# Chunked attention and a wide feed-forward on one core: dense turned weights, quarter-size value tiles, and keys and queries interleaved by GpSimd ahead of the transpose

## The chip, the cores and the metric

The kernel runs on one core of a Trainium2 chip. The core has TensorE (PE in the profile, with PEld for its weight loads), VectorE (DVE), ScalarE (ACT), GpSimd (POOL) and SyncE (SP), each of which works through its own instructions in program order and waits on semaphores for the others. DMAs are issued from the POOL and SP queues. The metric is device time in microseconds: 256.27 us is the median of three runs before the change (255.0 to 256.6).

## The reference

There are 4 batches, 8 heads, 768 positions and a head size of 64. Attention works in chunks of 32 queries. Each chunk sees 8 memory slots, 16 positions to its left, its own 32 and 8 to its right, that is 64 keys:

```
scores = (q_c @ [mem_k, k_ctx].T) / 8
a      = exp(scores - max) / sum
out_c  = a @ [mem_v, v_ctx]
```

The 8 heads side by side make a row x of 512 features. It is then normalized and passed through a feed-forward layer of width 2048: `x + relu(((x - mean) / std * g) @ w1) @ w2`. Inputs and output are float32; the kernel multiplies in float16.

## The kernel before

The unit of attention work is a tile t of 128 tokens (four chunks, all heads); a batch has 6 tiles, 24 in all. The feed-forward takes two tiles at a time, a "unit" u of 256 tokens, 12 units in all. While PE does the feed-forward of unit u, the attention of tiles 2u+2 and 2u+3 is woven in between.

**One attention tile** goes through these helpers.
- `qk(t)`: `qk_products` makes 32 small matmuls (line 294) of 64 rows by 32 columns, whose positions in the array repeat with period four, into one PSUM bank. `below_max` (lines 304, 305) takes the maximum and subtracts it on VectorE, `weights` (line 311) takes the exponential on ScalarE, into `P`.
- `pt(t)`: four transposes of `P` (line 321), then two copies (line 330), one on VectorE and one on ScalarE. They put the two 64-row halves into `PTz`, a tile twice as large whose other half is zero, so that a 128-row matmul can serve two chunks at once.
- `val(t)`: `val_products` makes 16 matmuls (line 336) of 128 rows by 64 columns against `V`, into the PSUM tile `two`. `tokens` (lines 345, 346, 352) divides by the sum and gives the mean on VectorE, `shift` (line 359) subtracts the mean on GpSimd into `xn`.
- `turn_x(t)`: four transposes of `xn` (line 388), and a multiplication by g on VectorE into `xT` (line 394). `root(t)`: a sum of squares on ScalarE and, on GpSimd, the reciprocal root `rstd` (lines 378, 382).

**The feed-forward of a unit** is 8 calls of `up` (line 407: 8 matmuls of 256 columns each, then a ReLU on ScalarE, line 415) and 7 of `down7` (line 472: 8 matmuls of 256 columns, then an addition on VectorE, line 479). `down7` computes a 2 by 2 block product with 7 products in place of 8, for which VectorE makes sums of activations (`r_sum`, line 468, four per unit) and, once, sums of weights (`w2_sum`, line 453). Unit u holds up(u) and down7(u-1). The first units use the plain `down` (line 423).

**Keys and queries** of a batch are loaded by two DMAs of the POOL queue (`load_octets`, line 117, called by `load_kq`) into `raw` tiles: 96 partitions of 8 positions each, all heads. They have to be turned, head size onto partitions, before `qk` can use them. `turn` (line 232) takes a pair of heads: 16 transposes of 96 rows by 64 columns, one head in the upper half of the array's columns and the other in the lower. `to_stream` (line 245, two copies) puts keys into `KT`, and `to_rows` (line 252, one copy) puts queries into `QD`. `turn_k` and `turn_q` do it for the head pair j, so a batch has four of each. The values of a batch come in small DMAs of the POOL queue (`load_v_group`, lines 125 and 130, for batches 0 and 1; `load_v_head`, lines 139 and 144, later) straight into `V`, and `v_shared` and `v_mem` (lines 161, 166) copy rows within `V` by DMAs of the SP queue.

**The order of work** is written out by hand. Up to unit 2 it is a list of calls ("the prologue": batch 0, both first units, then `down(0, 0)` to `down(0, 7)` with the four `turn_k` of batch 1 between them). From unit 2 on, a plan holds for each unit u and step 0 to 15 what is called ahead of that step's dense product; even steps end with `up(u, step/2)`, odd ones with `down7(u-1, step//2)`, or with `down(1, step//2)` in unit 2. Step 15 has no dense product from unit 3 on. All engines get their instructions in the order of this plan, so a GpSimd copy or a DMA issue stands in the POOL queue where the plan calls it.

In the plan, unit u has qk of its two tiles at steps 0 and 2, pt at 4 and 7, val at 6 and 9, turn_x at 11 and 14, root at 12 and 14 (in unit 2 everything but turn_x and root is four steps later). The keys and queries of batch b (2 or 3) are loaded at step 5 of unit 3b-4 and turned at steps 8, 9, 12 and 13 of units 3b-3 and 3b-2.

**PSUM:** from unit 2 on, scores, transposes and turns share the two banks `one` in turn (`slot`); `up` has two banks, `down7` two, `two` takes the last two.

## Time and profile before

| | |
|---|---|
| median of three timed runs | 256.27 us (255.0 to 256.6) |
| span of the profiled execution, first to last instruction | 255.3 us |
| mean granted TensorE clock | 0.971 |
| busy: PE, PEld, DVE, ACT, POOL | 235.8, 192.9, 176.0, 122.0, 94.4 us |
| instructions | 8286 |

The profile gives the profiled execution's span and no time around it; the median of the timed runs is 1.0 us above that span. Units without turns last 16.2 to 16.7 us in it (for instance 197.3 to 213.9), units with turns 18.6 to 19.1 us (143.5 to 162.1).

A row of a group gives line, engine and operation, out<-in, partitions x elements and type, the count, then the busy time and the mean ns of one, and the idle time of the engine ahead of them with what ended it. A row of the timeline gives start and length in us, then the same names, and in brackets the idle time before it and its releaser. Matmuls overlap in the pipeline, so the distance from one group's start to the next group's start tells more than a group's length.

### The profile page before, as it was taken

Reading aid. Unit: us, or ns where it says so; the run is one execution under the profiler, and the core shown is the slowest. Engines: PE = TensorE matmul, PEld = TensorE weight load, DVE = VectorE, ACT = ScalarE, POOL = GpSimd, SP = SyncE. Lnnn points to the kernel's source line nnn. Section 1 sums busy time; section 2 is a strip of 40 time slices with the busy share of each in tenths; the row PEclk is TensorE's granted clock in tenths of the full one; section 3 lists DMA queues with packets and bytes.
Section 4 is the critical chain, followed back from the end, with each engine's and each line's share of the span. In section 5 each row is a group of like instructions: output and inputs, shape, how many; then the busy total and the mean of one; then the engine's idle time right before and its main releaser. Section 6 shows DMA issues by size and latency. Waiting matters only on the chain.

```text
span 255.3 us, 8286 instructions
## 1 busy us (share of the span) xinstructions
PE 235.8 (92%) x3611; PEld 192.9 (76%) x3611; DVE 176.0 (69%) x390; ACT 122.0 (48%) x226; POOL 94.4 (37%) x164
## 2 busy tenths in 40 slices
PE   8697978999999989999999999999999999999983
PEld 7353656786566778888789878878889888899972
DVE  7535574757597598697696687687775966856272
ACT  2225456578345445545644464554555444653310
POOL 8394332016991296741322638712113022121000
PEclk9959995999999999999999999999999999999999
DMA  6989999932999987974196569933101002011022
GB/s 82 139 94 207 208 215 206 202 27 17 60 172 143 198 103 46 103 101 70 65 155 114 104 42 58 135 70 61 57 3 51 34 3 82 3 43 43 3 82 83
DMA packets 45816, 23.50 MB, mean 92 GB/s; under 512 B 33492, under 2 KB 41140, under 8 KB 45732
## 3 DMA queue, kind: packets, MB, share of 16 engines
q0 software_dynamic: 40672, 14.70, 49.2%
q1 hardware_dynamic: 5108, 8.28, 11.1%
q8 instruction: 28, 0.46, 0.8%
q14 instruction: 8, 0.07, 0.1%
HBM read 29.46 MB, written 6.29 MB: 140 GB/s over the span
## 4 chain that ended last, share of the span: by engine, by line
PE 69%; DVE 18%; ACT 4%; DMA 4%; issue 3%; DVEq 0%; ACTq 0%; POOLq 0%
PE upb L407 28%; PE dnb L472 18%; PE dnb L423 5%; DVE RS L468 4%; PE one L232 4%; DMA raw<-in_k_dram 4%; PE two L336 4%; DVE nmx L304 3%; DVE sub L305 3%; DVE xs L479 3%; PE one L294 2%; PE one L388 2%; ACT PTz L330 2%; PE upb L542 2%; DVE T L453 1%
## 5 line engine op out<-in xcount | busy, mean ns | idle before, releaser
L407 PE MATMUL upb<-xT,w1c 128*128 128x256 f16 x768 | 101.3, 276 | 1.2 <-DVE xT L394 0.9
L407 PEld LDWEIGHTS <-w1c 128*128 128x128 f16 x768 | 80.0, 115 | 5.5 <-DVE xT L394 1.4
L415 ACT ACTIVATE rT<-upb 128x512 f16<-128x512 f32 x92 | 54.6, 593 | 56.9 <-PE upb L407 56.7
L479 DVE SCALAR_TENSOR_TENSOR xs<-dnb,rstd,xs 128x256 f32<-128x256 f32 x70 | 33.7, 481 | 24.3 <-PE dnb L472 23.1
L359 POOL TENSOR_SCALAR xn<-xs,nmean 128x512 f16<-128x512 f32 x18 | 12.4, 691 | 76.6 <-DVE nmean L352 36.8
L472 PEld LDWEIGHTS <-RS 128*128 128x128 f16 x320 | 30.0, 98 | 4.3 <-DVE RS L468 0.7
L311 ACT ACTIVATE P<-sub 128x512 f16<-128x512 f32 x24 | 15.2, 632 | 35.0 <-DVE sub L305 34.9
L472 PE MATMUL dnb<-T,RS 128*128 128x256 f16 x240 | 30.9, 273 | 0.8 <-DVE xs L479 0.8
L472 PEld LDWEIGHTS <-rT 128*128 128x128 f16 x240 | 23.1, 98 | 2.6
L472 PE MATMUL dnb<-w2c,rT 128*128 128x256 f16 x160 | 20.6, 273 | 0.0
L394 DVE TENSOR_TENSOR xT<-one,g_col 128x512 f16<-128x512 f16 x22 | 15.1, 687 | 7.4 <-PE one L388 7.2
L232 PEld LDWEIGHTS <-raw 96*64 96x64 f16 (+2 forms) x576 | 13.5, 110 | 8.6 <-issue 5.8
L378 POOL TENSOR_SCALAR veps<-ssq 128x1 f32<-128x1 f32 x24 | 5.4, 227 | 36.2 <-ACT sq L374 36.0
L374 ACT ACTIVATE sq<-xs,nmean 128x512 f16<-128x512 f32 x24 | 17.3, 719 | 0.2
L346 DVE CUSTOM_DVE_ANT_1 xs<-two,rec 128x512 f32<-128x512 f32 x24 | 16.6, 691 | 0.8
L468 DVE TENSOR_TENSOR RS<-rT 128x1024 f16<-128x1024 f16 x20 | 13.7, 686 | 4.9 <-ACT rT L415 4.9
L423 PE MATMUL dnb<-w2c,rT 128*128 128x512 f16 x64 | 16.3, 380 | 0.0
L336 PEld LDWEIGHTS <-PTz 128*64 128x64 f16 x384 | 8.5, 114 | 10.2 <-ACT PTz L330 6.0
L304 DVE TENSOR_REDUCE nmx<-one 128x8 f32<-128x512 f32 x21 | 14.4, 684 | 2.1 <-PE one L294 2.0
L305 DVE TENSOR_TENSOR sub<-one,nmx 128x512 f32<-128x512 f32 x21 | 14.5, 691 | 0.7
L336 PE MATMUL two<-V,PTz 128*64 128x65 f16 x384 | 11.1, 202 | 4.1 <-ACT PTz L330 3.3
L382 POOL TENSOR_TENSOR rstd<-veps,mhalf 128x1 f32<-128x1 f32 x24 | 13.3, 554 | 2.0
(118 smaller groups left out, 321.4 us busy)
## 6 DMA issues: line engine op xcount, KB each, us to landing
out_dram<-xs SPq DMA_DIRECT2D x23, 256.0 KB, 2.0
raw<-in_k_dram POOLq DMA_DIRECT2D x4, 768.0 KB, 9.8
raw<-in_q_dram POOLq DMA_DIRECT2D x3, 768.0 KB, 14.8
w1c<-in_moe_w_ch_dram POOLq DMA_DIRECT2D x2, 1024.0 KB, 13.3
w2c<-in_moe_w_ch_dram POOLq DMA_DIRECT2D x4, 512.0 KB, 22.7
V<-in_v_dram POOLq DMA_DIRECT2D x16, 77.0 KB, 3.1
V<-in_v_dram POOLq DMA_DIRECT2D x15, 56.0 KB, 4.1
V<-memv SPq DMA_DIRECT2D x6, 120.0 KB
```

What stands on the lines that cost most here:

```text
L232: nc.tensor.matmul(out=pv[64 * par : 64 * par + 64, n * r : n * r + n], lhsT=src[lo : lo + n, heads + par, r, :], rhs=identity[lo : lo + n ...
L304: nc.vector.tensor_reduce(out=m, in_=scores, axis=AX.X, op=ALU.max)
L305: nc.vector.tensor_tensor(out=s.rearrange("p (c k) -> p c k", c=8), in0=scores, in1=free(m, 0, [[1, 8], [0, 64]]), op=ALU.subtract,)
L336: nc.tensor.matmul(out=two[64 * gg : 64 * gg + 64, 128 * h : 128 * h + 65], lhsT=PTz[t % 3][:, 4 * (h // 2) + 2 * gg + h % 2, :, :], rhs=V ...
L346: nc.vector.tensor_tensor_reduce(out=x.rearrange("p (h d) -> p h d", h=H), in0=free(two, 0, [[128, 8], [1, 64]]), in1=free(r, 0, [[1, 8], ...
L374: nc.scalar.activation(out=sq, in_=xs[t % 9], func=ACTF.Square, bias=nmean[t % 6], scale=1.0, accum_out=ssq[i],)
L407: nc.tensor.matmul(out=p[:, 256 * hb : 256 * hb + 256], lhsT=free(w1c[hc // 8][:, dt, :], 512 * (hc // 4 % 2) + hc % 4, [[4, 128]]), rhs=x ...
L415: nc.scalar.activation(out=o, in_=i, func=ACTF.Relu)
L423: nc.tensor.matmul(out=p, lhsT=rT[u % 2][:, hc, 128 * i : 128 * i + 128], rhs=w2c[hc // 4][:, hc % 4, :], start=(hc == 0), stop=(hc == 15),)
L468: nc.vector.tensor_tensor(out=RS[k], in0=a, in1=b, op=op)
L472: nc.tensor.matmul(out=p[:, 0:256], lhsT=left[:, n, :], rhs=right(n), start=(n == 0 and not add), stop=(n == 7), skip_group_check=add,)
L479: nc.vector.scalar_tensor_tensor(out=x, in0=p[:, 0:256], scalar=rstd[t % 9], in1=x, op0=ALU.mult, op1=ALU.add,)
```

## The change

1. `PTz` (three tiles of 128 x 1024 with zeros) becomes `PT` (three of 128 x 512). `pt` ends with one copy of all 128 partitions on ScalarE. The memsets of the zeros go.
2. `val_products` makes 32 matmuls of 64 rows by 32 columns in place of 16 of 128 by 64. Their positions in the array repeat with period four, as those of `qk_products` do.
3. In the plan, the scores of tile t+2 stand right behind val of tile t (steps 4 and 8), that is, a unit earlier than before; pt follows at steps 11 and 14 and val only in the next unit.
4. For batches 1 to 3, `mix` copies a pair of heads on GpSimd from `raw` into one of four `mixed` tiles (96 partitions, 8 x 128 elements, the two heads next to each other). `turn_mixed` then makes 8 transposes of 96 rows by all 128 columns in place of 16 by 64 columns.
5. The plan moves what belongs to it: batch 1 has four mixes behind its first value loads and four more between the `down` calls, where three of its four `turn_q` stand now as well; `w2_sum` is spread out; the loads of batches 2 and 3 are called at step 0 of unit 3b-4, their mixes from step 12 of that unit to step 7 of the next, all their turns at steps 1, 2, 5, 6, 10, 11, 13 and 15 of unit 3b-3. The value loads start at step 6; `load_v_ends`, `v_shared` and `v_mem` follow at steps 6 and 10 of unit 3b-2.

```diff
-    PTz = [sb.tile([128, 16, 2, 32], FP16, name=f"PTz{i}") for i in range(3)]
+    PT = [sb.tile([128, 4, 128], FP16, name=f"PT{i}") for i in range(3)]
+    mixed = [sb.tile([128, 8, 128], FP16, name=f"mixed{i}") for i in range(4)]
...
+    def mix(b, which, j):
+        src, m = raw[RAW[b][which]], mixed[(2 * j + which) % 4]
+        nc.gpsimd.tensor_copy(
+            out=m[0:96, :, :].rearrange("p r (a d) -> p r a d", a=2),
+            in_=free(src[0:96], 1024 * j, [[64, 8], [512, 2], [1, 64]]),
+        )
+
+    def turn_mixed(which, j):
+        p, src = slot(), mixed[(2 * j + which) % 4]
+        pv = as16(p)
+        for r in range(8):
+            nc.tensor.matmul(
+                out=pv[:, 96 * r : 96 * r + 96], lhsT=src[0:96, r, :],
+                rhs=identity[0:96, 0:96], is_transpose=True, start=True, stop=True,
+            )
+        return pv
...
     def turn_k(b, j, engine):
-        to_stream(KT[b % 2], turn(raw[RAW[b][0]], 2 * j), j, engine)
+        pv = turn_mixed(0, j) if b else turn(raw[0], 2 * j)
+        to_stream(KT[b % 2], pv, j, engine)
     def turn_q(b, j, engine):
-        to_rows(b, turn(raw[RAW[b][1]], 2 * j), j, engine)
+        to_rows(b, turn_mixed(1, j), j, engine)
...
-        z = PTz[t % 3]
-        src = pv.rearrange("p (c q) -> p c q", c=16)
-        for y in range(2):
-            rows = slice(64 * y, 64 * y + 64)
-            copy_on(engines[y])(out=z[rows, :, y, :], in_=src[rows, :, :])
+        copy_on(engine)(out=PT[t % 3].rearrange("p j q -> p (j q)"), in_=pv)
...
             for gg in range(2):
-                nc.tensor.matmul(
-                    out=two[64 * gg : 64 * gg + 64, 128 * h : 128 * h + 65],
-                    lhsT=PTz[t % 3][:, 4 * (h // 2) + 2 * gg + h % 2, :, :],
-                    rhs=V[b % 2][:, 2 * tt + gg, h, 0:65],
-                    start=True, stop=True, tile_position=(0, 64 * gg),
-                )
+                for y in range(2):
+                    rows, col = slice(64 * y, 64 * y + 64), 64 * gg + 32 * y
+                    q0 = 64 * gg + 32 * (h % 2)
+                    nc.tensor.matmul(
+                        out=two[col : col + 32, 128 * h : 128 * h + 65],
+                        lhsT=PT[t % 3][rows, h // 2, q0 : q0 + 32],
+                        rhs=V[b % 2][rows, 2 * tt + gg, h, 0:65],
+                        start=True, stop=True, tile_position=(64 * y, col),
+                    )
...
     for g in range(2):
         load_v_group(1, g)
+    for j in range(2):
+        mix(1, 0, j)
+        mix(1, 1, j)
...
+    mem_cols(KT[1], memKT[:, 4:8, :], True)
     down(0, 0)
     val(5, "A")
+    turn_k(1, 0, "A")
+    mix(1, 0, 2)
     turn_x(4)
     down(0, 1)
-    mem_cols(KT[1], memKT[:, 4:8, :], True)
+    turn_q(1, 0, "A")
+    mix(1, 1, 2)
+    w2_sum(0)
     down(0, 2)
     turn_x(5)
+    turn_k(1, 1, "A")
+    mix(1, 0, 3)
     down(0, 3)
-    root(4)
+    turn_q(1, 1, "A")
+    mix(1, 1, 3)
+    w2_sum(1)
     for g in range(6, 9):
         load_v_group(1, g)
-    turn_k(1, 0, "V")
     down(0, 4)
+    root(4)
+    turn_k(1, 2, "V")
+    down(0, 5)
     root(5)
     for g in range(9, NG):
         load_v_group(1, g)
-    turn_k(1, 1, "A")
-    down(0, 5)
-    turn_k(1, 2, "V")
+    turn_q(1, 2, "A")
     down(0, 6)
-    turn_k(1, 3, "A")
+    turn_k(1, 3, "V")
     down(0, 7)
...
-    for j in range(4):
-        at(2, j, turn_q, 1, j, "AV"[j % 2])
+    at(2, 0, turn_q, 1, 3, "A")
+    at(2, 4, qk, 6)
+    at(2, 4, qk, 7)
+    at(2, 7, pt, 6)
+    at(2, 8, pt, 7)
...
+            for step, t in ((4, a), (8, c)):
+                at(u, step, val, t)
+                if t + 2 < 2 * NP:
+                    at(u, step, qk, t + 2)
+            at(u, 8, turn_x, a)
+            at(u, 7, root, a)
+            at(u, 12, turn_x, c)
+            at(u, 11, root, c)
+            if u < NP - 2:
+                at(u, 11, pt, a + 2)
+                at(u, 14, pt, c + 2)
...
-        at(u0 - 1, 5, load_kq, b)
+        at(u0 - 1, 0, load_kq, b)
+        for n, (j, which) in enumerate((j, w) for j in range(4) for w in range(2)):
+            w, step = ((-1, 12), (-1, 13), (0, 0), (0, 1), (0, 3), (0, 5), (0, 6), (0, 7))[n]
+            at(u0 + w, step, mix, b, which, j)
+            step = (1, 2, 5, 6, 10, 11, 13, 15)[n]
+            if which:
+                at(u0, step, turn_q, b, j, "A")
+            else:
+                at(u0, step, turn_k, b, j, "V")
         for h in range(H):
+            w, step = divmod(6 + 2 * h, 16)
             for part in range(2):
-                at(u0, 2 * h, load_v_head, b, h, part)
+                at(u0 + w, step + part, load_v_head, b, h, part)
...
-        at(u0 + 1, 15, mem_cols, KT[b % 2], memKT[:, 4 * b : 4 * b + 4, :], True)
+        at(u0 + 1, 0, mem_cols, KT[b % 2], memKT[:, 4 * b : 4 * b + 4, :], True)
```

(`u0` is 3b-3. In unit 2 the values of tiles 6 and 7 stand at steps 9 and 11, the scores of tiles 8 and 9 at steps 12 and 15, and their pt at steps 2 and 3 of unit 3.)

More of the change, by code (lines that the diff above doesn't have):

```diff
@@ L315, in qk, with pt @@
         weights(t)
-    def pt(t, engines="VA"):
+    def pt(t, engine="A"):
         p = slot()
@@ L595 @@
     nc.vector.tensor_copy(out=memv0, in_=memv32)
-    for i in range(2):
-        nc.vector.memset(PTz[i][64:128, :, 0, :], 0.0)
-        nc.vector.memset(PTz[i][0:64, :, 1, :], 0.0)
     nc.vector.memset(mhalf, -0.5)
```

39 lines of the change are left out of this document (14 added, 25 removed).

## The prediction

> **What bounds the kernel now.** I read the busy times first, then PE's timeline of one unit with turns (unit 6, then the start of 7), then the waits of PE from 90 to 230 us.
>
> ```profile
> PE 235.8 (92%) x3611; PEld 192.9 (76%) x3611; DVE 176.0 (69%) x390; ACT 122.0 (48%) x226; POOL 94.4 (37%) x164
> ```
> ```profile
> 157.18 1.04 PE L472 MATMUL dnb<-w2c,RS 128*128 128x256 f16 x8
> 158.14 0.53 PE L232 MATMUL one<-identity,raw 96*64 96x96 f16 x16
> 158.61 1.06 PE L407 MATMUL upb<-xT,w1c 128*128 128x256 f16 x8
> 159.60 0.53 PE L232 MATMUL one<-identity,raw 96*64 96x96 f16 x16
> 160.06 1.05 PE L472 MATMUL dnb<-T,rT 128*128 128x256 f16 x8
> ...
> 166.70 1.04 PE L407 MATMUL upb<-xT,w1c 128*128 128x256 f16 x8
> 167.57 1.04 PE L472 MATMUL dnb<-T,RS 128*128 128x256 f16 x8
> 169.19 0.44 PE L336 MATMUL two<-V,PTz 128*64 128x65 f16 x16 [0.58 <-ACT PTz L330]
> 169.56 1.07 PE L407 MATMUL upb<-xT,w1c 128*128 128x256 f16 x8
> ```
> ```profile
> PE two L336 <- ACT PTz L330: 3.3, 7, 0.6
> PE upb L407 <- DVE xT L394: 0.9, 1, 0.9
> PE one L294 <- DVE KT L214: 0.7, 2, 0.3
> ```
>
> PE is busy 92% of the span. A dense group that another dense group follows takes 0.87 us from start to start (166.70 to 167.57). So PE's order is nearly the time, and there are three things to gain: what small groups cost, what entering them costs, and the waits. Two turns with two dense groups take 157.18 to 160.06, 2.88 us, less 2 x 0.87: **0.57 us a turn**, of which 0.09 is in the dense group ahead (157.18 to 158.14 is 0.96) and 0.03 behind. The val group takes 0.37 us (169.19 to 169.56); with the same entry and exit it costs about 0.50. The waits that PE shows from unit 3 to unit 11 add up to 3.3 + 0.9 + 0.7 = 4.9 us.
>
> **The change part by part.**
>
> *Values.* Twice as many matmuls, each a quarter of the array. The nearest row is scores, which have this count, size and pattern of positions:
>
> ```profile
> 33.80 0.41 PE L294 MATMUL one<-KT,QD 64*32 64x64 f16 x32
> 34.05 0.45 PE L294 MATMUL dnb<-KT,QD 64*32 64x64 f16 x32
> 34.43 0.48 PE L232 MATMUL dnb<-identity,raw 80*64 80x80 f16 x16
> ```
>
> One takes 0.38 us alone (34.05 to 34.43), and the 16 larger matmuls took 0.37: nothing gained or lost by the split itself (0.1 either way kept for the range, 24 tiles). But of two such groups in a row the first takes only 0.25 (33.80 to 34.05). With val at 0.50 and scores at 0.35 + 0.13, the two apart cost 0.98; side by side 0.25 + 0.35 + 0.13 = 0.73. The plan has 16 such pairs (units 2 to 9): 16 x 0.25 = **-4.0 us**.
>
> *Turns.* Eight transposes by all columns in place of 16. The trace has no 96 x 128 one that streams 96 columns. Matmuls of 128 columns of weights that stream 64 take 0.94/32 = 29 ns (below); the dense ones that stream 256 take 0.87/8 = 109 ns. A line through both gives 42 ns for 96.
>
> ```profile
> 5.40 1.11 PE L548 MATMUL upb<-zeros 128*128 128x64 f16 x32
> 6.34 1.89 PE L542 MATMUL upb<-zeros 128*128 128x512 f16 x8
> ```
>
> So 8 x 42 = 0.34 us, and no entry and exit, since the shape of the array stays. I take 0.35, 24 turns: 24 x 0.22 = **-5.3 us**. Bounds: at the 29 ns of the shorter stream 0.23 us, at the 109 ns of the longer 0.87, which would lose 7 us; the line lies far nearer the first.
>
> *Waits.* Val now comes two steps behind its pt in unit 2 and eight from unit 4 on, and the first scores of a batch four steps behind mem_cols, so all **-4.9 us** can go. What is late next is worked out below. The copy on VectorE leaves its queue:
>
> ```profile
> L330 DVE COPY PTz<-one 64x512 f16<-64x512 f16 x19 | 7.8, 410 | 0.6
> L346 DVE CUSTOM_DVE_ANT_1 xs<-two,rec 128x512 f32<-128x512 f32 x24 | 16.6, 691 | 0.8
> L304 DVE TENSOR_REDUCE nmx<-one 128x8 f32<-128x512 f32 x21 | 14.4, 684 | 2.1 <-PE one L294 2.0
> L305 DVE TENSOR_TENSOR sub<-one,nmx 128x512 f32<-128x512 f32 x21 | 14.5, 691 | 0.7
> L245 DVE COPY KT<-one 128x576 f16<-128x576 f16 x10 | 7.5, 748 | 0.0
> L245 DVE COPY KT<-one 128x192 f16<-128x192 f16 x10 | 3.6, 357 | 1.3 <-PE one L232 1.1
> ```
>
> ScalarE keeps its copy, only larger in partitions, so this is nothing on PE's path. In a unit without turns I walked the plan with these durations: behind val, VectorE needs about 1.2 us (0.69 for line 346 and three short ones) plus 0.68 + 0.69 for the scores, and the bank of scores is wanted again three steps or 3.1 us later. That fits, by 0.3 us.
>
> *Two banks in a unit with turns.* Units 3 and 6 now hold eight turns each. The same walk there finds PE three times at a bank that VectorE hasn't emptied: at step 6 (the subtraction of step 4, 0.5 us), at step 10 (that of step 8, 0.6) and at step 11 (the key copies of step 10, 0.75 + 0.36, 0.8 us). Together 1.9, taken as 2.0 us a unit: **+4.0 us**. Below, none if VectorE runs ahead; above 6, if mixes delay VectorE as well.
>
> *Mixes.* GpSimd has no such copy in the trace. Its nearest rows are a fill of the same type, and, for what VectorE does to GpSimd, three of the timeline:
>
> ```profile
> L529 POOL MEMSET V<- 128x1536 f16 x1 | 1.4, 1402 | 0.0
> ```
> ```profile
> 56.70 0.19 POOL L378 TENSOR_SCALAR veps<-ssq 128x1 f32<-128x1 f32 x1 [5.17 <-ACT sq L374]
> 90.42 0.68 DVE L468 TENSOR_TENSOR RS<-rT 128x1024 f16<-128x1024 f16 x1
> 90.53 0.63 POOL L378 TENSOR_SCALAR veps<-ssq 128x1 f32<-128x1 f32 x1
> ```
>
> 1402/1536 is 0.91 ns an element; 1024 elements and some 0.15 us to start are 1.1 us. Bounds: half of that if two elements go at once, twice if reading and writing add up. 90.53 shows that GpSimd can be held: the same line takes 0.19 us at 56.70, and here it ended with VectorE's sum. The Trainium skill, "SBUF — State Buffer", section "Who interferes with whom", says that a VectorE instruction with two SBUF inputs and a GpSimd instruction that reads SBUF lock each other out whole. The row agrees for one direction; the other, a mix that holds a sum, no row shows, and by the page each collision would cost VectorE up to one mix.
>
> *Where POOL's queue decides.* A mix waits for its DMA to land, and everything behind it in POOL's queue waits too.
>
> ```profile
> 33.18 0.77 POOL L117 DMA_DIRECT2D raw<-in_q_dram  x1 [5.04 <-PE one L232]
> 59.39 1.03 PE L423 MATMUL dnb<-w2c,rT 128*128 128x512 f16 x4
> 62.35 0.79 POOL L125 DMA_DIRECT2D V<-in_v_dram  x1
> 76.31 0.77 POOL L117 DMA_DIRECT2D raw<-in_k_dram  x1
> ```
> ```profile
> raw<-in_q_dram POOLq DMA_DIRECT2D x1, 768.0 KB, 19.3
> raw<-in_k_dram POOLq DMA_DIRECT2D x1, 768.0 KB, 10.6
> raw<-in_q_dram POOLq DMA_DIRECT2D x1, 768.0 KB, 14.8
> raw<-in_q_dram POOLq DMA_DIRECT2D x1, 768.0 KB, 10.5
> ```
>
> Batch 1's queries land at 33.2 + 19.3 = 52.5; the first four mixes end near 56, inside the idle 5.2 us ahead of 56.70: free. From 62.35 to 76.31 POOL issues value loads nearly without a gap. The next four mixes stand behind the first three pairs of these, at about 66.3 to 70.7. PE comes to turn_k(1, 2) at about 66.3 (from `down(0, 0)` at 59.39 on, by the prices above) and waits for the first until 67.4: **+1.1 us**. And all loads behind them move by 4 x 1.1: although batch 2's keys are called five steps earlier, they are issued not at 76.3 but near 80, right behind the last value loads. Of the landing times I take those of this place (second and third row, with the DMAs full), less 1 us since part of the traffic is past: keys at 89.6 to 90.7, queries 94.4 to 95.7. PE enters unit 3 at about 89.0 (71.5 at the end of the prologue, then 16 x 0.87 of dense work and 3.6 of attention). There turn_k(2, 0), at 89.9, waits for a mix that ends near 91.2, and turn_q(2, 0) for one that ends near 96.2. Less the work in between, PE stands still 1.4 + 3.5: **+4.9 us**. Bound below: with the last row (batch 3's queries, issued into idle queues) 1.3 us. Batch 3 itself, called at the start of unit 5 and mixed twelve steps (11.5 us) later, is in time by that row. Behind the wait in POOL's queue stand root(7) and xn of tile 8, which are due only at the end of unit 3.
>
> *Sum.* -4.0 - 5.3 - 4.9 + 4.0 + 1.1 + 4.9 = **-4.2 us** on the span of 255.3. The page gives no time around the span; the median of the timed runs is 1.0 above it, and I carry that: 256.3 - 4.2 = **252 us**. About 1% is what a measurement of this kernel can tell from no change.
>
> **Rivals.**
>
> *The clock halves behind the wait.*
>
> ```profile
> 32.20:39.00 6.80, 4.36 (x177) 3.56 (x176) 5.12 (x10) 4.46 (x10) 2.03 (x3) 1.00 1.08 215
> 39.00:45.90 6.90, 6.30 (x80) 4.83 (x81) 3.56 (x11) 3.62 (x7) 1.31 (x2) 0.51 1.16 204
> 18.50:25.40 6.90, 5.15 (x57) 2.49 (x55) 3.67 (x9) 3.19 (x5) 3.32 (x5) 1.00 1.17 207
> ```
>
> With PE idle for 2.4 of 6.8 us (first row) the granted clock is 0.51 in the next 6.9; idle for 1.75 (last row) it stays 1.00. A wait of 4.9 us within 6.5 would likely be over the limit. The price is half of 6.8 us, 3.4, less some 0.8 of bank waits that a slower PE doesn't meet: 2.6 us, 252 + 2.6 = **255 us**. Against it: the wait comes in two pieces, and a boundary between them could leave each short. The Trainium skill, "TensorE: Matmul & The Clock Gate", section "What's actually happening", speaks of a free-running window that must be idle; by that, pieces of 1.4 and 3.5 us may not trip it. The rows here halve the clock at less than one whole idle window, so I trust them more.
>
> *The loads land in time.* At the lower bound the wait is 1.3 in place of 4.9: **248 us**, with no halved clock. For it: fewer transfers share the DMAs than in 76 to 92 us of before. Against it: the last value loads go right ahead.
>
> *GpSimd's copy is dear.* The case on the other side. At 2.2 us a mix, the four behind the value loads last to 75, the loads of batch 2 are issued near 84.6, and its queries are ready near 101.5 in place of 96: +5.5, then the halved clock +2.6, a late xn in unit 6 (+1.3) and sums held by longer mixes (+1): 252 + 10 = **262 us**. It decides from about 1.6 us a mix, with the clock halved. For it: three-level source addresses and a shared port. Against it: 0.91 ns an element in the row.
>
> *Whole turns aren't cheaper.* If a transpose of 96 columns takes 60 to 70 ns, a turn costs what it did: 252 + 4 = **256 us**.
>
> **How the numbers follow.** Forecast 252 (251 to 253.5): 0.30. Halved clock 255: 0.23. Loads in time 248: 0.20. Dear copies 262: 0.17. Turns no cheaper 256: 0.10. Faster by over 1% means under 253.7: the forecast, the loads in time and a little of the halved clock, 0.52. Slower means over 258.8: the dear copies and a little more, 0.20. Within 1%: 0.28. The range takes in 248 with 2 us for bank waits that don't come, and up to 261, short of the whole of the dear case: 246 to 261.
>
> **What would show it.** In the after profile: the scores groups right behind val start 0.25 us after it, and val has no row that waits for PT. Turns (eight matmuls of 96 x 128) take 0.34 us to the next start. Copies on POOL last 1.1 us. Units 4, 5, 7 and 8 last about 15.4 us, unit 6 about 20. The waits of PE name the mixed tiles at the start of unit 3, and POOL waits there for raw's DMA. The clock rows show whether 0.5 follows. The prediction is wrong if mixes take over 1.6 us, if units without turns stay above 16, or if unit 3 shows no wait.

## The result, and the profile after

The changed kernel takes **253.06 us** (median of 11 runs, 250.6 to 253.8); the kernel before took 255.40 (median of 11 runs too). The ratio is 0.988, with a 95% interval of 0.985 to 0.992: the gain is clear of the noise, and small. The profiled execution took 253.46 us and spans 251.5. The forecast was 252 us, within 246 to 261.

The page of the changed kernel, busy times and GpSimd's new copies:

```profile
PE 230.8 (92%) x3803; PEld 194.6 (77%) x3803; DVE 166.6 (66%) x358; ACT 119.6 (48%) x228; POOL 120.7 (48%) x188
L261 POOL COPY mixed<-raw 96x1024 f16<-96x1024 f16 x24 | 26.5, 1134 | 11.2 <-DMA raw<-in_q_dram 5.7
```

PE lost 5 us of work and is still busy for 92%. POOL gained 26 us. PE's timeline in unit 6 (start, length, and the idle time before it with its releaser in brackets):

```profile
145.21 0.51 PE L271 MATMUL one<-identity,mixed 96*128 96x96 f16 x8
145.55 1.04 PE L492 MATMUL dnb<-w2c,rT 128*128 128x256 f16 x8
...
148.61 0.42 PE L356 MATMUL two<-V,PT 64*32 64x65 f16 x32
148.87 0.44 PE L315 MATMUL one<-KT,QD 64*32 64x64 f16 x32
149.24 1.06 PE L427 MATMUL upb<-xT,w1c 128*128 128x256 f16 x8
...
152.62 0.50 PE L271 MATMUL one<-identity,mixed 96*128 96x96 f16 x8 [1.09 <-DVE sub L326]
```

A turn takes 0.34 us (145.21 to 145.55), and the scores start 0.26 behind the values (148.61 to 148.87), both as forecast. The waits of PE from 55 us to the end (total, times, longest):

```profile
PE one L271 <- POOL mixed L261: 4.3, 2, 2.3
PE two L356 <- DMA V<-memv: 2.4, 3, 1.3
PE one L271 <- DVE sub L326: 1.7, 3, 1.1
...
PE one L271 <- DVE KT L246: 0.6, 2, 0.3
```

No row names PT any more. In its place stand mixes (copies by `mix` on GpSimd, into a `mixed` tile), and a releaser that no step of the prediction has: `V<-memv`, the memory rows that `v_mem` copies into V.

**Where the time went**, from the starts of PE's groups in both timelines. Up to the first `down`: 59.39 to 57.58, -1.8 us. From there to unit 3: +2.9, of which about 1 us (an estimate: two score groups at 0.48) is the scores of two tiles that stand ahead of unit 3 now. Unit 3 (90.29 to 112.91, 22.6 us): +3.5. Units 4 and 7, which have lost their turns: -3.5 each. Unit 6 (20.5 us): +1.9. Units 5 and 8: +0.5 together. From unit 9 to the end: -3.8, since these scores are no longer among the last. Together -3.8 us on the span.

The first of these was not in the sum. VectorE's timeline in the start, before and after:

```profile
19.66 0.42 DVE L330 COPY PTz<-dnb 64x512 f16<-64x512 f16 x1 [2.78 <-PE dnb L321]
20.00 0.67 DVE L304 TENSOR_REDUCE nmx<-dnb 128x8 f32<-128x512 f32 x1
```
```profile
16.60 0.68 DVE L325 TENSOR_REDUCE nmx<-dnb 128x8 f32<-128x512 f32 x1
```

Before, VectorE's half of the weights' copy stood in its queue ahead of the second tile's maximum, and waited 2.78 us for PE to turn the first tile's weights. The whole copy is on ScalarE now, and the maximum is 3.4 us earlier. The start itself varies from profile to profile (last section). Of the nine profiles whose start is of the same kind, the kernel before alone has its first `up` at 28.7 us, and the eight with the whole copy on ScalarE at 26.7 to 27.5.

Now the places where PE waits for mixes in the changed kernel: PE, then GpSimd, then windows of time. A row of a window gives its start, end and length, the busy time (and instructions) of PE, PEld, DVE, ACT and POOL, PE's granted clock, the busy share of the DMA engines and the GB/s that they moved.

```profile
63.31 1.03 PE L443 MATMUL dnb<-w2c,rT 128*128 128x512 f16 x4
66.28 0.72 PE L271 MATMUL one<-identity,mixed 96*128 96x96 f16 x8 [1.94 <-POOL mixed L261]
...
95.22 0.51 PE L271 MATMUL one<-identity,mixed 96*128 96x96 f16 x8 [2.33 <-POOL mixed L261]
```
```profile
64.69 4.48 POOL L261 COPY mixed<-raw 96x1024 f16<-96x1024 f16 x4
...
94.13 1.04 POOL L261 COPY mixed<-raw 96x1024 f16<-96x1024 f16 x1 [2.90 <-DMA raw<-in_q_dram]
```
```profile
59.40:66.20 6.80, 4.94 (x49) 2.77 (x46) 5.85 (x9) 5.27 (x11) 6.63 (x11) 1.00 0.83 53
66.20:69.90 3.70, 3.62 (x22) 2.05 (x23) 1.02 (x2) 0.52 (x1) 3.70 (x6) 0.54 0.02 4
88.00:96.00 8.00, 5.67 (x89) 4.48 (x87) 6.77 (x10) 4.93 (x11) 3.42 (x6) 1.00 0.68 156
```

In the prologue PE needs 2.97 us from 63.31 on instead of 0.87, a wait of 2.1, and then works at about half the clock for 3.7 us (0.54). In unit 3 GpSimd waits for the queries' DMA, and PE for GpSimd, but the clock stays at 1.00.

### The profile page after: what moved, and what is told of

The parts are those of the page before. It is cut to its first block, busy times and chain, and to the rows that moved or that the text cites. A ratio compares the mean times of both kernels' runs of the same rounds, so it can differ in the third digit from the quotient of the medians.

```text
span 251.5 us, 8668 instructions
## 1 busy us (share of the span) xinstructions
PE 230.8 (92%) x3803; PEld 194.6 (77%) x3803; DVE 166.6 (66%) x358; ACT 119.6 (48%) x228; POOL 120.7 (48%) x188
## 4 chain that ended last, share of the span: by engine, by line
PE 59%; DMA 15%; DVE 10%; POOL 9%; issue 3%; ACT 2%; DVEq 0%; POOLq 0%; ACTq 0%
PE upb L427 25%; PE dnb L492 19%; DMA V<-memv 6%; DMA raw<-in_q_dram 6%; DMA raw<-in_k_dram 4%; POOL V L126 3%; PE upb L562 2%; PE two L356 2%; POOL V L131 2%; POOL mixed L261 2%; DVE xs L366 2%; PE one L408 2%; DVE xs L499 2%; PE one L271 2%; PE one L315 2%
## 5 line engine op out<-in xcount | busy, mean ns | idle before, releaser
L427 PE MATMUL upb<-xT,w1c 128*128 128x256 f16 x768 | 99.3, 275 | 0.1
L427 PEld LDWEIGHTS <-w1c 128*128 128x128 f16 x768 | 81.1, 115 | 3.3 <-issue 0.6
L435 ACT ACTIVATE rT<-upb 128x512 f16<-128x512 f32 x92 | 53.4, 593 | 38.4 <-PE upb L427 38.0
L379 POOL TENSOR_SCALAR xn<-xs,nmean 128x512 f16<-128x512 f32 x18 | 13.7, 759 | 38.3 <-PE upb L427 20.7
L261 POOL COPY mixed<-raw 96x1024 f16<-96x1024 f16 x24 | 26.5, 1134 | 11.2 <-DMA raw<-in_q_dram 5.7
L488 DVE TENSOR_TENSOR RS<-rT 128x1024 f16<-128x1024 f16 x20 | 15.1, 756 | 9.9 <-ACT rT L435 9.9
L271 PEld LDWEIGHTS <-mixed 96*128 96x128 f16 x192 | 10.9, 100 | 10.2 <-POOL mixed L261 5.1
L325 DVE TENSOR_REDUCE nmx<-one 128x8 f32<-128x512 f32 x21 | 14.4, 685 | 5.6 <-PE one L315 5.6
L443 PE MATMUL dnb<-w2c,rT 128*128 128x512 f16 x64 | 17.7, 401 | 0.0
L271 PE MATMUL one<-identity,mixed 96*128 96x96 f16 x160 | 10.3, 208 | 6.7 <-POOL mixed L261 4.3
L126 POOL DMA_DIRECT2D V<-in_v_dram x16 | 11.8, 737 | 6.9 <-DMA w1c<-in_moe_w_ch_dram 3.2
## 6 DMA issues: line engine op xcount, KB each, us to landing
raw<-in_q_dram POOLq DMA_DIRECT2D x3, 768.0 KB, 15.9
```

The source lines that it names most:

```text
L126: nc.gpsimd.dma_start(out=V[b % 2][72 : 72 + n, g, :, 0:64], in_=dram(v, b * H * HS + (64 * g + 16) * D, [[64, n], [HS, H], [1, 64]]),)
L261: nc.gpsimd.tensor_copy(out=m[0:96, :, :].rearrange("p r (a d) -> p r a d", a=2), in_=free(src[0:96], 1024 * j, [[64, 8], [512, 2], [1, 64]]),
L271: nc.tensor.matmul(out=pv[:, 96 * r : 96 * r + 96], lhsT=src[0:96, r, :], rhs=identity[0:96, 0:96], is_transpose=True, start=True, stop=True,)
L427: nc.tensor.matmul(out=p[:, 256 * hb : 256 * hb + 256], lhsT=free(w1c[hc // 8][:, dt, :], 512 * (hc // 4 % 2) + hc % 4, [[4, 128]]), rhs=x ...
L435: nc.scalar.activation(out=o, in_=i, func=ACTF.Relu)
L443: nc.tensor.matmul(out=p, lhsT=rT[u % 2][:, hc, 128 * i : 128 * i + 128], rhs=w2c[hc // 4][:, hc % 4, :], start=(hc == 0), stop=(hc == 15),)
```

## The experiments

In the table, "from the first `down`" is the span less the start of that product in the same profile; it leaves the start out, whose length varies (last section). Each ratio is against the runs of the kernel before that were taken along with that kernel's runs (their medians lie between 254.8 and 255.4 us).

| kernel | median us | ratio to before (95%) | from the first `down`, us |
|---|---|---|---|
| before | 255.40 | 1 | 195.9 |
| changed | 253.06 | 0.988 (0.985 to 0.992) | 193.9 |
| e_denseonly | 251.56 | 0.985 (0.979 to 0.991) | 193.6 |
| e_rawturns | 251.02 | 0.979 (0.971 to 0.988) | 192.1 |
| e_apart | 256.29 | 1.002 (0.998 to 1.007) | 197.3 |
| e_mixtwice | 270.19 | 1.056 (1.048 to 1.064) | 212.7 |
| e_memrows | 252.54 | 0.989 (0.983 to 0.996) | 194.1 |
| e_mixfirst | 254.97 | 0.998 (0.993 to 1.002) | 192.9 |
| e_loads2 | 257.36 | 1.004 (1.000 to 1.009) | 201.2 |
| e_ahead | 253.80 | 0.995 (0.991 to 0.999) | 194.1 |
| e_order | 257.84 | 1.010 (1.006 to 1.014) | 199.5 |
| e_rawmem | 247.54 | 0.967 (0.961 to 0.972) | 188.9 |
| e_hybrid | 247.32 | 0.969 (0.964 to 0.975) | 187.5 |

The profiled runs of e_mixfirst (251.96 us, the fastest of ten) and of e_rawmem and e_hybrid are among the fastest of theirs, those of e_loads2, e_order and e_mixtwice (258.65, 259.06, 271.81) among the longest; the ratio is the measure, the last column tells where.

The theory: the dense weights and the values beside the scores pay, and the mixes give back what the cheaper turns earn, because GpSimd has them in one queue with the DMA issues. The first rival: the loads alone are late, and with them sooner the whole change pays. The second: VectorE's two banks and the lock of the shared port.

### The parts, one at a time

**e_denseonly**, the kernel before with the first two points of the change:

```diff
-            copy_on(engines[y])(out=z[rows, :, y, :], in_=src[rows, :, :])
...
+        copy_on(engine)(out=PT[t % 3].rearrange("p j q -> p (j q)"), in_=pv)
...
```

`val_products` is that of the change, the order of work that of before.

> The kernel before with one part of the change alone: the turned weights dense, one ScalarE copy in place of two copies by ScalarE and VectorE, values by quarter-size tiles. The plan, the turns and the loads are those of before. Theory (a late copy, not the tile size, is what this part removes): in the start the second unit's maximum no longer stands behind VectorE's copy, so the first product of the feed-forward starts up to 1.7 us sooner, and PE's 3.3 us of waits for the zero-padded weights fall to about 1.5, because the one copy of all rows takes longer than the half did: 250 to 252.5 us, 0.98 to 0.99 of before. Rival (the recorded working: the copy that leaves VectorE is nothing on PE's path, and the waits go only because values stand two units behind their weights): within 0.5 us of before, 0.998 to 1.002.

Measured 0.985: this part alone is worth as much as the whole change, within the intervals. Part of the difference between the two profiles is the varying start, but the last column of the table leaves that out: 193.6 us against 195.9 before. A row of its waits of PE:

```profile
PE two L335 <- ACT PT L326: 1.4, 5, 0.3
```

The waits for the weights fall from 3.3 to 1.4 us although val stands where it stood. The theory of a late copy holds, and the recorded "nothing on PE's path" falls: the copy that the prediction left out of its sum was on the path.

**e_rawturns**, the changed kernel without mixes:

```diff
-        pv = turn_mixed(0, j) if b else turn(raw[0], 2 * j)
-        to_stream(KT[b % 2], pv, j, engine)
+        to_stream(KT[b % 2], turn(raw[RAW[b][0]], 2 * j), j, engine)
...
-            at(u0 + w, step, mix, b, which, j)
...
```

`turn_q` is changed alike, and the eight mixes of batch 1 go too.

> The changed kernel with the copies on GpSimd left out and its turns made as before, 16 transposes of 96 rows by 64 columns straight from the loaded tiles, in the places of the changed plan. Theory: the 24 turns cost 0.57 in place of 0.34 us, +5.5, while the waits for the copies (1.9 and 2.3), the half clock in the prologue (1.7) and the sums that a copy holds (1.1 at unit 6) go, -7.0; the net is near -1.5, span about 250, ratio 0.98 to 0.985, so the copies earn nothing as they are placed. Rival (whole turns are the larger gain): the span rises by 2 us or more, ratio 0.995 or above, because something else is late in their place.

```profile
145.08 0.53 PE L233 MATMUL one<-identity,raw 96*64 96x96 f16 x16
145.54 0.63 PE L426 MATMUL upb<-xT,w1c 128*128 128x256 f16 x4
```

Its turn takes 0.46 us and makes the dense groups beside it 0.1 longer, the old price. With 24 dearer turns it is no slower than the changed kernel: 251.0 us against 253.1, though the two intervals touch (0.971 to 0.988, 0.985 to 0.992). So **as placed, the mixes earn nothing**. That they cost more than they save is clear from e_rawmem below: with the memory rows sooner and no mixes it has 0.961 to 0.972, and e_memrows and e_ahead, with the memory rows sooner and the mixes, have 0.983 to 0.996 and 0.991 to 0.999.

**e_apart**, the changed kernel with the scores one dense product behind the values:

```diff
-                    at(u, step, qk, t + 2)
+                    at(u, step + 1, qk, t + 2)
```

> The changed kernel with the scores of units 3 to 8 issued one dense product after the values instead of right behind them. By the recorded price (0.25 us a pair) PE loses 0.25 x 12 = 3 us: 256 us, 1.000 of before. By the traces of both kernels the product ahead of a narrow group is 0.10 us longer and the one behind it 0.03 us, so parting a pair costs one more entry and exit, 0.13 us x 12 = 1.6 us: 254.6 us, 0.995. In the trace: scores at 0.34 to 0.35 us instead of 0.37, and the product between at 0.99 to 1.00 us instead of 0.87 to 0.90.

The time is nearer the recorded price; its rows in unit 4 are not:

```profile
117.81 1.04 PE L492 MATMUL dnb<-w2c,rT 128*128 128x256 f16 x8
118.77 0.42 PE L356 MATMUL two<-V,PT 64*32 64x65 f16 x32
119.13 1.07 PE L427 MATMUL upb<-xT,w1c 128*128 128x256 f16 x8
...
120.13 0.41 PE L315 MATMUL one<-KT,QD 64*32 64x64 f16 x32
120.47 1.05 PE L492 MATMUL dnb<-T,RS 128*128 128x256 f16 x8
```

Five groups, from the dense one ahead of val to the one behind the scores, take 0.96 + 0.36 + 1.00 + 0.34 + 0.89 = 3.55 us, against 0.97 + 0.25 + 0.38 + 0.90 + 0.87 = 3.37 in unit 4 of the changed kernel. The second pair gives 0.14, and the whole unit 0.34 for its two. So a pair is worth **0.17 us**, not 0.25. The plan has 14 pairs, in units 3 to 9 (in unit 2 the scores stand away from the values), and they make 2.4 of the 3.4 us between the two profiles. The rest is waits: PE's for mixes are 6.0 us here (3 times) against 4.3, and those for memory rows 1.7 against 2.4.

**e_mixtwice**, each mix made twice:

```diff
     def mix(b, which, j):
+        mix_once(b, which, j)
+        mix_once(b, which, j)
```

> The changed kernel with each of the 24 mixes made twice, so 27 us more of copies on GpSimd. If mixes set PE's pace wherever they stand (the recorded rival of a dear copy, 262 us at 2 to 2.2 us a mix): 261 to 266 us, 1.02 to 1.04 of before. If they count only where GpSimd is late (four mixes in the prologue, some three in unit 3) and are hidden in unit 6: 4.5 + 3 us and some clock, 259 to 261 us, 1.014 to 1.022. If GpSimd's time is idle time: under 255 us.

```profile
PE one L275 <- POOL mixed L265: 11.3, 4, 6.0
PE one L412 <- POOL xn L383: 5.2, 2, 3.2
```

270 us, above all three: 17 us more for 24.5 us of copies (51.0 against 26.5). GpSimd's time isn't idle time. Of these, 7 us are in the waits for mixes and 5.2 in a new one, for xn, which GpSimd computes behind the mixes; the rest isn't placed.

### The late transfers

**e_memrows** issues the memory rows sooner, and nothing else:

```diff
+    v_mem(1)
     mem_cols(KT[1], memKT[:, 4:8, :], True)
     down(0, 0)
...
-    at(2, 0, v_mem, 1)
...
-        at(u0 + 1, 10, v_mem, b)
+        at(u0, 2, v_mem, b)
```

> The changed kernel with one thing moved: the DMAs that copy the memory rows into V are called at step 2 of the unit that turns the batch (batch 1: ahead of the first `down`), not behind the shared rows eight steps after it. Theory: these DMAs, of 192 small packets, land last before the first values of each batch; PE's waits for them (0.8, 0.25 and 1.3 us in units 2, 5 and 8, 2.4 in all) go and nothing else is late, so the span falls from 251.5 to about 249.2 and the ratio to the kernel before from 0.988 to about 0.979. Rival: the shared rows, which are issued later now, land as late; then the same waits stay under the other name and the ratio stays at 0.986 to 0.988.

The waits for the rows are gone, and PE's largest wait is a new one, while GpSimd waits for batch 1's queries (PE, then POOL):

```profile
69.56 0.82 PE L271 MATMUL one<-identity,mixed 96*128 96x96 f16 x8 [5.21 <-POOL mixed L261]
```
```profile
56.06 3.03 POOL L261 COPY mixed<-raw 96x1024 f16<-96x1024 f16 x3 [6.16 <-DMA raw<-in_q_dram]
```

In the changed kernel these mixes start at 52.80. That the rows' transfer, issued into the same stretch, is what held the queries up is the likely reading; no run separates it. The prologue took back what units 2, 5 and 8 gained.

**e_mixfirst** puts value groups 3 to 5 behind the second four mixes:

```diff
-    for g in range(3, 6):
-        load_v_group(1, g)
...
-    for g in range(6, 9):
+    for g in range(3, 9):
         load_v_group(1, g)
```

> The changed kernel with the value loads of groups 3 to 5 of batch 1 moved behind the second four GpSimd copies, so that the order in POOL's queue changes and its total does not. Theory (POOL's queue decides): the wait of 1.9 us among the `down` products goes, and the half clock behind it (3.4 us at 0.5, worth 1.7) goes too, but batch 2's keys and queries are issued at the same time as now, near 78.6 and 79.4, so PE comes to unit 3 some 3.6 us earlier and waits there for the copies 2.3 + 3.6 = about 6 us; the span falls by under 1 us, and the half clock may come at unit 3 instead. Rival (the prologue's wait is a loss of its own): the span falls by 3 to 3.6 us, to about 248, ratio 0.974.

The prologue's wait and its halved clock are gone, and PE comes to the first values of unit 2 four microseconds sooner (77.1 against 81.2). There it waits:

```profile
79.12 0.42 PE L356 MATMUL two<-V,PT 64*32 64x65 f16 x31 [2.04 <-DMA V<-memv]
...
90.79 0.52 PE L271 MATMUL one<-identity,mixed 96*128 96x96 f16 x8 [0.74 <-POOL mixed L261]
94.88 0.51 PE L271 MATMUL one<-identity,mixed 96*128 96x96 f16 x8 [2.48 <-POOL mixed L261]
```

It turns batch 2's first queries at 94.88; in the changed kernel it was 95.22. In this profile the prologue's wait was paid for already: what binds up to here is the landing of batch 2's loads. The waits for mixes in unit 3 are 3.2 us, not the 6 of the recorded theory. The median of 254.97 us (0.993 to 1.002) is above the changed kernel's, and this profile, of the fastest run, doesn't show why; that stays open.

**e_loadsahead** and **e_loads2** issue these loads sooner. In e_loadsahead the keys' load stood too early: its turns of batch 0's values read batch 2's keys, and PE waited 29.3 us for them. So it computes something else, and at 283 us it tells nothing of the theory.

```diff
+    load_octets(2, k, 2, 0, 96, 0)
     up(0, 3)
...
     mix(1, 1, 3)
+    load_octets(0, q, 2, 0, 96, 0)
...
```

> The changed kernel with batch 2's key load moved in POOL's queue to right behind the first four copies of batch 1 and its query load to right behind the second four, ahead of the value loads of groups 6 to 11. Theory: the copies of batch 2 are then in time and the 2.3 us that PE waits at unit 3 go; the value loads of groups 6 to 11 come 0.8 us later and are still in time for tiles 9 and 10; span about 249, ratio about 0.978. Rival: the DMAs are full from 70 to 92 us, so that the 1.5 MB ahead of them hold the value rows and the memory rows; then PE waits for V in unit 2 or 3 by 2 us or more and the ratio stays at 0.985 or above.

e_loads2 has the keys' load behind value group 2 and the queries' behind the last mix:

```diff
     load_v_group(1, 2)
+    load_octets(2, k, 2, 0, 96, 0)
     up(1, 4)
...
     mix(1, 1, 3)
+    load_octets(0, q, 2, 0, 96, 0)
     w2_sum(1)
...
```

> The changed kernel with batch 2's loads issued sooner: the keys' behind the value loads of group 2 in the prologue (the octets that held batch 0's values are free by then), the queries' right behind the last mix of batch 1. Theory (PE waits at the start of unit 3 because GpSimd issues the two loads late): the 2.3 us wait for the mixed queries in unit 3 and the gap ahead of it go, 2.5 to 4 us less, and the prologue's wait for mixes grows by at most the one issue of 0.8 us: 249.5 to 251.5 us, 0.977 to 0.985 of before. Rival (the DMA engines are the bound, not the issue): batch 1's value loads or the mixes come later by as much, and the time stays at 252.5 to 254 us, 0.989 to 0.995.

Its waits (PE's, by line; then PE's timeline):

```profile
PE one L271 <- POOL mixed L261: 4.4, 1, 4.4
```
```profile
86.29 0.62 PE L356 MATMUL two<-V,PT 64*32 64x65 f16 x31 [1.72 <-DMA V<-memv]
```

Unit 3's wait for mixes is gone, as the theory says: the one that is left is the prologue's, and it has grown from 1.9 to 4.4 us. PE also waits 2.1 and 1.7 us in unit 2, and its clock is at half for longer (0.54 from 85 to 90 us). The time is 257.4 us, above both recorded ranges.

**e_ahead** puts all three changes together and orders the memory rows behind the first shared rows:

```diff
...
+    v_shared(1, 0, 4)
+    v_mem(1)
...
-        at(u0 + 1, 10, v_mem, b)
+        at(u0, 2, v_mem, b)
```

> The changed kernel with every transfer that PE was seen to wait for issued sooner: batch 2's loads as in e_loads2, the second four mixes of batch 1 ahead of the value loads of groups 3 to 8, and the memory rows of the values behind the first shared rows of batch 1, and for batches 2 and 3 one unit sooner. Theory (the waits for mixes, 4.3 us, for the memory rows, 2.4 us, the 1.7 us of halved clock behind the first of them and about 1 us that PE had drained ahead of it are all late issues and add up): 244 to 247 us, 0.955 to 0.968 of before. Rival (the transfers share engines that are full, so each that is pulled ahead makes another late): 250 to 253 us, 0.98 to 0.99.

The waits for mixes are gone altogether, and what the rival describes is there: other transfers are late. The time, 253.8 us, is a little above its range (POOL, then PE):

```profile
72.23 0.73 POOL L126 DMA_DIRECT2D V<-in_v_dram  x1
74.96 0.58 POOL L131 DMA_DIRECT2D V<-in_v_dram  x1 [2.01 <-DMA raw<-in_q_dram]
```
```profile
81.36 0.21 PE L356 MATMUL two<-V,PT 64*32 64x65 f16 x1 [3.70 <-DMA V<-memv]
83.44 0.63 PE L356 MATMUL two<-V,PT 64*32 64x65 f16 x31 [1.87 <-DMA V<-memv]
```

The value loads now stand behind two loads of 768 KB. GpSimd stands 2.0 us at the issue of one of them; the profile names the queries' load as what ended it. The memory rows, which PE waits for here, stand in SP's queue behind shared rows that need these values, and are issued at 76.1 us, against 74.5 in the changed kernel. So **e_order** asked for the order of first use: values first, then batch 2's loads, and the groups that only unit 4 reads at the end; and batch 3's loads a unit sooner, its mixes off the steps of the sums.

```diff
-    for g in range(3, 6):
-        load_v_group(1, g)
...
-    for g in range(6, 9):
+    for g in range(3, 8):
         load_v_group(1, g)
+    v_shared(1, 0, 4)
+    v_mem(1)
+    load_octets(2, k, 2, 0, 96, 0)
+    load_octets(0, q, 2, 0, 96, 0)
...
-    for g in range(9, NG):
+    for g in range(8, NG):
         load_v_group(1, g)
...
+            at(u0 - 2, 6, load_kq, b)
...
+            if b > 2:
+                w, step = ((-1, 8), (-1, 10), (-1, 12), (-1, 14), (0, 6), (0, 7), (0, 8), (0, 9))[n]
...
```

> The changed kernel with its mixes, reordered after what e_ahead and e_loads2 showed (there big loads stood ahead of the value loads that the next units need). GpSimd's queue is now: second four mixes of batch 1, value groups 3 to 7, batch 2's keys and queries, and only then groups 8 to 11, which no unit reads before unit 4. The memory rows follow the first shared rows. Batch 3's loads go one unit sooner and its mixes are kept off the steps at which VectorE forms the sums RS. Theory (late issues, each at its own place): the prologue's 3 us and its 1.7 us of halved clock go, the waits for the memory rows, 2.4 us, go, unit 3's wait falls from 2.3 to about 1, unit 6's 1.1 us falls to 0.3 with RS at 0.7 us instead of up to 1.5: 245 to 248 us, 0.960 to 0.972 of before. Rival (a mixed kernel is bound by its queue and its transfers whatever their order): 250 to 253 us, 0.98 to 0.99, with a wait of 3 us or more left in unit 2 or 3.

Every wait that it aimed at is gone (mixes, memory rows, unit 6's 1.09), and one new wait is longer than all of them:

```profile
86.06 0.62 POOL L126 DMA_DIRECT2D V<-in_v_dram  x1 [4.36 <-DMA raw<-in_k_dram]
90.24 0.58 POOL L131 DMA_DIRECT2D V<-in_v_dram  x1 [3.56 <-DMA raw<-in_q_dram]
90.85 1.36 POOL L379 TENSOR_SCALAR xn<-xs,nmean 128x512 f16<-128x512 f32 x2
```
```profile
91.61 0.61 PE L408 MATMUL one<-identity,xn 128*128 128x128 f16 x4 [10.57 <-POOL xn L379]
```

The small loads behind the large ones stop GpSimd at their issue, for 4.4 and 3.6 us, and xn, which PE needs, stands behind them in the same queue. My forecast for it missed by 10 us, for the reason that e_ahead had already shown on a smaller scale. The recorded rival (bound by its queue and transfers) has the mechanism, and 257.8 us is above its range too.

Its unit 6 answers the question of the sums. VectorE's sums there in the changed kernel, then in e_order:

```profile
145.17 1.28 DVE L488 TENSOR_TENSOR RS<-rT 128x1024 f16<-128x1024 f16 x1 [1.24 <-ACT rT L435]
146.48 1.41 DVE L488 TENSOR_TENSOR RS<-RS,rT 128x1024 f16<-128x1024 f16 x1
149.13 0.68 DVE L488 TENSOR_TENSOR RS<-rT 128x1024 f16<-128x1024 f16 x1
```
```profile
153.31 0.69 DVE L488 TENSOR_TENSOR RS<-rT 128x1024 f16<-128x1024 f16 x1 [1.24 <-ACT rT L435]
154.04 0.69 DVE L488 TENSOR_TENSOR RS<-RS,rT 128x1024 f16<-128x1024 f16 x1
```

Five mixes run from 142.90 to 148.79 in the changed kernel, and the sums beside them take up to 1.41 us; moved apart they take 0.69, and PE's wait of 1.09 is not there.

So neither rival holds as far as it was tried. With batch 2's loads sooner the whole change doesn't pay in any of the three orders (e_loads2, e_ahead, e_order: 1.004, 0.995 and 1.010), and e_order has the sums away from the mixes as well.

### What beats both

**e_rawmem** is e_rawturns with e_ahead's memory rows:

```diff
...
+    v_shared(1, 0, 4)
+    v_mem(1)
...
-        at(u0 + 1, 10, v_mem, b)
+        at(u0, 2, v_mem, b)
```

> e_rawturns (the changed kernel's order without mixes, turns by head as before) with the memory rows issued as in e_ahead. Theory: its 2.7 us of waits for the memory rows go and no other wait takes their place, because nothing else of the queues moves: 247.5 to 249 us, 0.970 to 0.976 of before; so the best of the kernels without mixes. Rival (as in e_memrows, where the rows issued sooner put batch 1's queries off by 3.3 us): 250.5 to 252 us, 0.981 to 0.987.

247.5 us, 3.3% under the kernel before; its theory holds, and PE waits for no DMA behind the start. **e_hybrid** adds mixes for batch 3 alone, with e_order's places:

```diff
...
+        pv = turn_mixed(0, j) if b > 2 else turn(raw[RAW[b][0]], 2 * j)
...
-        at(u0 - 1, 0, load_kq, b)
+        at(*((u0 - 1, 0) if b < 3 else (u0 - 2, 6)), load_kq, b)
...
+            if b > 2:
+                at(u0 + w, step, mix, b, which, j)
```

> e_rawmem (turns by head, no mixes, memory rows issued sooner) with mixes for batch 3 alone, where e_order showed them to cost PE nothing: loads one unit sooner, mixes away from the RS sums. From the first turn of unit 6 to the end of its last PE needs 18.65 us in e_order and 19.8 us in e_rawmem, so 1.2 us less: about 246.3 us, 0.962 of before. Rival (a mix costs as much as it saves wherever it stands): 247 to 248 us, 0.967 or more, with a new wait in unit 5 or 6 (in e_order unit 5 waited 1.0 us for shared rows behind the sooner loads).

From its first turn (140.34) to the end of its last, unit 6 takes 18.65 us, as expected, and 1.2 less than in e_rawmem, with no new wait. The time of 247.3 us lies in the rival's range, not at the theory's 246.3. The timed runs don't tell the two apart: 0.969 (0.964 to 0.975) against 0.967 (0.961 to 0.972). That the gain reaches the time is not shown.

## Why the prediction was right, and where its steps were not

The sum was -4.2 us on the span and the profiles show -3.8; around the span lie 2.0 us (253.46 less 251.5) where I carried 1.0. The measured 253.06 us is 1.1 above the forecast, well within the range; that the gain is over 1%, as forecast, is likely and not certain, since the interval reaches 0.8%. But the gains and the losses are each made of other terms than I gave.

- *Turns*, -5.3: right. 0.34 us with no longer neighbours, against 0.46 and 0.1 more around it in e_rawturns.
- *Values*, -4.0: the mechanism is right, the size is not. "The two apart cost 0.98", and 0.73 together; e_apart and the changed kernel have 0.94 and 0.76 (3.55 and 3.37, less 3 x 0.87). The count is off too: "16 such pairs (units 2 to 9)" takes in unit 2, where the scores stand away from the values, so there are 14. At 0.17 a pair the term is -2.4. That the split itself costs nothing (0.36 us against 0.37) is right.
- *Waits*, -4.9: all of them went, though 1.9 of it comes without moving anything (e_denseonly). "This is nothing on PE's path" was the step that failed: in the start VectorE's copy stood ahead of work that the path needs, 1.8 us up to the first `down`. What is late next was missed as well: `v_mem` of batch 2, which the change moves back by two steps behind its value loads, is issued at 123.8 us instead of 113.6, has landed at 132.4, and is wanted at 132.2 where it was 134.0 before. Batch 3's goes the same way (issued at 176.2 instead of 168.9, wanted at 184.1 instead of 187.8). Batch 1's call didn't move; it is issued at 74.5 instead of 72.1 and wanted at 81.2 instead of 82.4. These are 2.4 us in three places, of a DMA that stands in no step of mine.
- *Two banks*, +4.0: it measured 0.6 in unit 3 and 1.7 in unit 6. The walk put VectorE too late in unit 3. In unit 6 it is the lock, which I had cited without a row for this direction; now there is one. The Trainium skill, "SBUF — State Buffer", section "Who interferes with whom", has it as an exclusive lock, whoever starts first. The sums agree: 0.68 us apart from mixes and up to 1.41 beside them.
- *Mixes*, 1.1 us each: right (1.134 in the mean).
- *Units without turns*: "about 15.4 us" holds for units 4, 5 and 7 (15.5, 15.9, 15.5), and "above 16" was named as a sign of being wrong. Unit 8 takes 17.0, of which 1.3 is the wait for memory rows. Unit 6 takes 20.5, where "about 20" was given.
- *POOL's queue*: the prologue's +1.1 was 2.1 us of waiting and 1.7 us of halved clock, because PE came there 2 us sooner than I had it (first `down` at 57.58, turns cheaper). Unit 3's +4.9 was 2.3, because PE, held up in the prologue and by the memory rows, came there later than 89.0: the keys had landed. The loads themselves were issued at 78.6 and 79.4 us, near the 80 that I gave. e_mixfirst shows that the two waits hang together: take the first away and the second is longer, 3.2 us for 2.3.

So 14.2 us of gains were forecast and about 14.4 are there (2.4 + 5.3 + 4.9 + 1.8, a gain that was too large and one that was left out); 10.0 of losses, and 10.8 are there (2.1 + 1.7 + 2.4 + 2.3 + 2.3: the prologue's wait and its clock, memory rows, two banks, unit 3). That the sums agree is partly luck.

Of the rivals, the halved clock came, at another place and for 1.7 us instead of 2.6. The dear copy was no case (1.1 us), but by e_mixtwice, whose two copies of a mix take 2.1 us, it would have cost about 17, not 10. The loads did not land in time. "Whole turns aren't cheaper" did not come: they are.

## What to carry to other kernels

An engine that both issues DMAs and computes has one order for both: a load moved up delays all that is issued behind it, and while earlier transfers are under way the engine itself can stop at an issue (4.4 us in e_order), with the computing behind it. Cheaper work on the busiest engine (the turns) was worth nothing here as long as its preparation came late out of such a queue; where it came in time (unit 6 of e_hybrid) it took 1.2 us less. Take a change of several parts apart: here one part alone was worth about the whole (1.5% against 1.2%), and the rest without the mixes, with the memory rows sooner, 3.3%.

## What the runs showed that was not expected

**The start has two lengths, and PE's own speed goes with them, not the first keys' DMA.** All kernels issue the first keys' load at 1.34 to 1.36 us, and it takes 8.2 to 9.3 us to land. Still, in some profiles PE waits 1.6 to 2.3 us for these keys and in others not at all. What differs is how fast PE goes through products with zeros that stand ahead of them. The same rows of the changed kernel and of e_rawturns:

```profile
5.44 1.11 PE L568 MATMUL upb<-zeros 128*128 128x64 f16 x32
6.39 1.89 PE L562 MATMUL upb<-zeros 128*128 128x512 f16 x8
```
```profile
5.72 1.89 PE L567 MATMUL upb<-zeros 128*128 128x64 f16 x32
7.42 3.48 PE L561 MATMUL upb<-zeros 128*128 128x512 f16 x8
```

The 32 products take 0.95 us from start to start in the first and 1.70 in the second, which is busy with them until the keys are there. Its granted clock reads 1.00 in these rows all the same, so that column alone doesn't show it. Behind a wait the clock is 0.50 from 12 to 15 us (nine profiles of ten; in the tenth, e_memrows, it stayed 1.00), and later again:

```profile
15.00:25.00 10.00, 9.64 (x148) 4.66 (x137) 5.22 (x14) 4.31 (x6) 6.46 (x10) 0.82 1.06 167
```
```profile
15.00:25.00 10.00, 9.41 (x127) 4.54 (x115) 6.56 (x15) 5.03 (x7) 6.48 (x10) 1.00 1.09 166
```

The first `up` starts at 26.7 to 28.7 us in the nine, and at 24.9 to 25.1 in the three that don't wait (e_denseonly, e_rawturns, e_loads2). Why PE is at one speed or the other there is open. At the first `down` the nine, the kernel before left out, are at 56.2 to 57.9 us and the three at 55.6 to 56.7, so about one microsecond of it is left. That is one reason why a single profile can't settle 1% here. It may also be why the kernel before, unchanged, ranges from 254 to 257 us: its spans go from about 252 us at a mean clock of 0.993 to about 255.5 at 0.970, with others in between, and the profiled run (255.3 us, 0.971) is one of the long ones. Where in the span the others lost their time isn't shown, since only this one has a profile.

**The clock halves sooner than I thought.** In the prologue PE was idle for 1.86 of 6.8 us, with no gap over 2.1, and the next 3.7 us ran at 0.54; in unit 3, idle for 2.33 of 8, it kept 1.00. By "TensorE: Matmul & The Clock Gate" of the Trainium skill, section "What's actually happening", a whole idle window of 3.4 us is needed. The prologue's rows contradict it. What tells the two places apart is open.

**An issue can stop GpSimd.** GpSimd stood for 4.4 and 3.6 us at the issue of small value loads (in e_order), with two of 768 KB and several small ones under way. The kernel before shows it already: its value loads at 35.3, 37.7, 40.2 and 42.6 us stood for 1.3 to 1.9 us each, until a load of `w1c` or `w2c` of the same queue had landed. That the queue is full then is the likely reading; how much fits was not tried.
